# Float64 weights to float32 in an mLSTM and MoE kernel: the three low bits made by ScalarE, two VectorE passes per weight tile

## The chip, the cores and the metric

The kernel runs on one core of a Trainium2 chip. A core has TensorE (matrix products; PE in the profile, its weight loads PEld), VectorE (DVE), ScalarE (ACT), GpSimd (POOL) and the queue of SyncE (SP) that issues transfers. Each executes its own instructions in order and waits on semaphores for the others. The metric is the device time of one execution in microseconds.

## The reference, cut to what matters

Per batch and head an mLSTM recurrence runs over 768 positions with head size 40; its outputs, 8 heads side by side (320 columns), go through a feed-forward layer with softplus:

```python
m_new = np.maximum(f_gate[:, :, t] + m, i_gate[:, :, t])
f_stab = np.exp(f_gate[:, :, t] + m - m_new)
i_stab = np.exp(i_gate[:, :, t] - m_new)
C = f_stab[...] * C + i_stab[...] * np.einsum('bhd,bhe->bhde', vt, kt)
n = f_stab[...] * n + i_stab[...] * kt
h_tilde = np.einsum('bhde,bhe->bhd', C, qt)
denom = np.maximum(np.abs(nq), 1.0)
y[:, :, t] = o * h_tilde / denom          # o = sigmoid(o_gate)
...
h = x @ w_in                              # 3072 x 320 by 320 x 2048
g = np.maximum(h, 0.0) + np.log1p(np.exp(-np.abs(h)))
return (g @ w_out).astype(np.float32)     # 2048 x 320
```

`w_in` and `w_out` arrive as float64, two 32-bit words for each weight. Every product of the feed-forward layer is made from float32 values split in two parts: a rounded part (`wih`, `woh`, `X[0:3]`, `gh`) and the rest (`wil`, `wol`, `X[3:6]`, `gl`); three products replace one.

## The kernel before, in words

**Tiles.** The tokens are cut into 24 steps of 128 (a batch and a chunk of 128 positions each, in the list `ORDER`), three steps to a tile of 384 tokens, so eight tiles `t`. The hidden layer is cut into 16 blocks `f` of 128. For each pair of tile and block, `products()` issues eight matmuls into `hp` (L971) and, two blocks later, nine into the three accumulators `po` (L939); ScalarE makes `gh` and the full softplus from `hp` (L845, L846) and VectorE the rest `gl` (L849).

**The recurrence.** For each step VectorE scans the decays (`pw`, L430, two scans over 128 x 512), TensorE makes the scores `sp` (L504), VectorE multiplies them in (L506). TensorE makes the chunk's contribution `cp` to the state (L481) from `vw`, which GpSimd makes (L457) from VectorE's weights `gw` (L451); VectorE adds it to the state `cn` (L486), which the next step of that batch reads (`ip` L528, `iq` L557). The first six steps ("plain") lead to token rows `x` (L550) that TensorE transposes into `xp` (L615, L617), ScalarE casts to `X` (L619) and VectorE subtracts (L621); later steps ("wide") come out transposed (`y` L560, `yq` L568).

**The weights.** Each of 16 weight tiles (eight of `w_in`, called `i`, and eight of `w_out`, called `o`; 128 partitions x 640 weights) is loaded raw into one of three buffers `wr` (`load_weights`, L221 to L227) and turned into float32 in `single` (L190 to L207). `hi_w` and `lo_w` are the upper and lower words, read with a stride of two words. ScalarE reads `hi_w` as a float32 and scales it by 2^-112 (`mag`, L198): that moves the exponent. VectorE takes the sign bit out of `hi_w` into `sg` (L201), ORs in `mag` shifted left by three (L203), and ORs in the three top bits of `lo_w` (L205). Then ScalarE casts the result to the rounded part (L236, L240 for `w_in`, L251 for `w_out`), and GpSimd subtracts that for the rest (L243, L245, L253). `sg` has three buffers, `mag` two.

**What sets the order.** `in_order()` fixes the order of instructions on each engine as they are written. They are written by a queue of generators keyed by the count of matmuls issued: `convert(u, i)` makes one step of `single` and of what follows it at each of the offsets `CW` (for `w_in`) or `CO` (for `w_out`), `fetch` loads the next raw tile. `single` has four steps before the change and four after, so each of them falls at the same count as before. All sixteen conversions end within the first quarter of the run; from then on the weights are resident. An instruction that waits holds up all those behind it on its engine.

The first tile's start is written out by hand in `first_tile()`, which calls the first conversion (`wparts`) between the steps of the recurrence.

Of the kernel before, what the change touches and what calls it, by code (L numbers as in the profile page):

```python
# [11 lines left out]
AF = mybir.ActivationFunctionType  # L12
ALU = mybir.AluOpType
# [26 lines left out]
def mlstm_moe_kernel(  # L40
# [10 lines left out]
    nc = tc.nc  # L51
# [138 lines left out]
    def single(src, n):  # L190

        if not words:
            return src
        lo_w, hi_w = src[:, :, :, 0], src[:, :, :, 1]
        shape = list(hi_w.shape)
        mag = stage.tile(shape, F32, tag="mag", bufs=MB, name=f"mag{n}")

        nc.scalar.activation(mag, hi_w.bitcast(F32), AF.Copy, scale=2.0**-112)  # L198
        yield
        sg = stage.tile(shape, U32, tag="sg", bufs=3, name=f"sg{n}")  # L200
        nc.vector.tensor_scalar(sg, hi_w, 0x80000000, None, op0=ALU.bitwise_and)  # L201
        yield
        nc.vector.scalar_tensor_tensor(sg, mag.bitcast(U32), 3, sg, op0=ALU.logical_shift_left, op1=ALU.bitwise_or)  # L203
        yield
        nc.vector.scalar_tensor_tensor(sg, lo_w, 29, sg, op0=ALU.logical_shift_right, op1=ALU.bitwise_or)  # L205
        yield
        return sg.bitcast(F32)  # L207

# [21 lines left out]
    def weights(u):  # L230

        cs = slice(u * 256, (u + 1) * 256)
        w = yield from single(raw[u, 0], f"i{u}")
        w2 = w[:, 0:4].rearrange("p (c j) f -> p c (j f)", c=2)
        los = []
        nc.scalar.copy(wih[:, 0:2, cs], w2)  # L236
        for i in range(2):
            c1 = slice((2 * u + i) * 128, (2 * u + i + 1) * 128)
            hi, lo = slice(i * 64, (i + 1) * 64), slice((1 - i) * 64, (2 - i) * 64)
            nc.scalar.copy(wih[hi, 2, c1], w[hi, 4])  # L240
            los.append((wih[lo, 2, c1], w[hi, 4], wih[hi, 2, c1]))
        yield
        nc.gpsimd.tensor_tensor(wil[:, :, cs], w2, wih[:, 0:2, cs], op=ALU.subtract)  # L243
        for d, x, y in los:
            nc.gpsimd.tensor_tensor(d, x, y, op=ALU.subtract)  # L245
        yield

    def weights_out(u):
        w = yield from single(raw[u, 1], f"o{u}")
        js = slice(2 * u, 2 * u + 2)  # L250
        nc.scalar.copy(woh[:, js, :], w)  # L251
        yield
        nc.gpsimd.tensor_tensor(wol[:, js, :], w, woh[:, js, :], op=ALU.subtract)  # L253
        yield
# [842 lines left out]
```

## Time and profile before

| | |
|---|---|
| three runs | 496.26, 500.42 and 500.45 us, median 500.42 |
| the profiled execution | 497.97 us, of which 496.3 between its first and last instruction (the span) |
| mean granted TensorE clock in it | 0.974 |
| busy in the span | TensorE 473.9 us (96%), weight loads 451.9, VectorE 336.3 (68%), GpSimd 223.4 (45%), ScalarE 205.8 (41%) |
| the five instruction lines that convert weights on VectorE and ScalarE | L198 12.6 us, L201 12.1, L203 16.5, L205 17.3; the casts L236, L240, L251 15.5 |

How to read the views in the prediction. A row of stretches gives the start and end of a stretch in us from the span's start, its length, then the busy us of PE, PEld, DVE, ACT and POOL (with the count of instructions that start in it), the granted clock (1.00 is full), the DMA share and GB/s. A row of a timeline gives start, duration, engine, line, operation, output and inputs, shape and count; the bracket is the idle time of that engine before it and what ended it. A grouped row gives busy us, mean ns and the idle time before. A row of a line gives the shortest, median and longest duration in ns. A row of waits gives the total, how often, and the longest.

### The profile page before, as it was taken

The numbers are of one execution on the slowest core, as the hardware profiler recorded it, in microseconds if no ns is written. First come the engines' busy times: TensorE is split into PE (matmuls) and PEld (weight loads), VectorE is DVE, ScalarE is ACT, GpSimd is POOL, SyncE is SP. The second block draws the span as 40 slices with busy tenths as digits, with TensorE's granted clock in tenths as the row PEclk, the third lists the DMA queues.
The fourth block names the chain that finished last, engine by engine and source line by source line (L and its number), as shares of the span: only waits on it lengthen the run. The fifth ranks groups of instructions, "written<-read, shape, count | busy, mean of one in ns | idle before, by whom it ended". The sixth has DMA issues, their size and how long they took to land.

```text
span 496.3 us, 9355 instructions
## 1 busy us (share of the span) xinstructions
PE 473.9 (96%) x3444; PEld 451.9 (91%) x3444; DVE 336.3 (68%) x533; ACT 205.8 (41%) x408; POOL 223.4 (45%) x303
## 2 busy tenths in 40 slices
PE   8988979798999989999999999999999999999996
PEld 8977878697998889999999999999999999999996
DVE  8788967888877576696587677578568657542211
ACT  2544515376424632536343534254352632333332
POOL 8256736666966324743365352643374344010000
PEclk9997978989999999999999999999999999999999
DMA  6936873769865877568856684569655572001001
GB/s 181 302 119 199 245 220 97 201 169 276 216 179 142 243 205 206 163 177 210 220 154 178 193 227 140 168 192 221 205 155 183 149 210 71 16 22 42 0 1 40
DMA packets 52991, 81.10 MB, mean 163 GB/s; under 512 B 7906, under 2 KB 31634, under 8 KB 52946
## 3 DMA queue, kind: packets, MB, share of 16 engines
q1 hardware_dynamic: 44738, 67.82, 49.0%
q0 software_dynamic: 4320, 8.26, 6.1%
q10 hardware_dynamic: 3888, 4.43, 2.8%
q8 instruction: 27, 0.44, 0.4%
q14 instruction: 18, 0.15, 0.1%
HBM read 52.38 MB, written 8.80 MB: 123 GB/s over the span
## 4 chain that ended last, share of the span: by engine, by line
PE 70%; DMA 12%; DVE 11%; issue 3%; ACT 2%; SPq 1%; POOL 0%; ACTq 0%; DVEq 0%; POOLq 0%
PE hp L971 31%; PE po L939 29%; PE yq L568 3%; PE sp L504 3%; DVE pw L430 3%; DMA wr<-in_w_in 3%; PE cp L481 2%; PE iq L557 2%; DMA wo<-in_w_out 2%; DMA out<-ob 1%; DMA sgp<-og 1%; DMA kst<-in_qk 1%; DMA fb<-fz_d 1%; DVE sgo L203 1%; DMA qst<-in_qk 1%
## 5 line engine op out<-in xcount | busy, mean ns | idle before, releaser
L971 PE MATMUL hp<-X,wih 128*128 128x384 f32 x768 | 185.3, 345 | 4.4 <-ACT X L619 3.0
L971 PEld LDWEIGHTS hp<-X,wih 128*128 128x128 f32 x768 | 133.8, 191 | 7.4 <-ACT X L619 3.4
L845 ACT ACTIVATE gh<-hp 128x384 fp32r<-128x384 f32 x128 | 62.7, 490 | 173.1 <-PE hp L971 154.5
L849 DVE TENSOR_TENSOR gl<-hp,gh 128x384 fp32r<-128x384 f32 x128 | 70.2, 549 | 58.1 <-ACT hp L846 57.8
L939 PE MATMUL po<-woh,gh 128*128 128x320 f32 x384 | 84.3, 318 | 0.1
L939 PE MATMUL po<-woh,gl 128*128 128x320 f32 x384 | 83.5, 312 | 0.1
L939 PE MATMUL po<-wol,gh 128*128 128x320 f32 x384 | 83.0, 316 | 0.0
L430 DVE TENSOR_TENSOR_SCAN pw<-fb,ident 128x512 f32<-128x512 f32 x48 | 73.2, 1565 | 0.1
L971 PE MATMUL hp<-X,wil 128*128 128x384 f32 x256 | 70.7, 349 | 0.3 <-POOL wil L243 0.3
L939 PEld LDWEIGHTS po<-woh,gh 128*128 128x128 f32 x384 | 66.8, 192 | 0.9 <-ACT gh L845 0.4
L939 PEld LDWEIGHTS po<-wol,gh 128*128 128x128 f32 x384 | 62.9, 191 | 1.0 <-issue 0.9
L939 PEld LDWEIGHTS po<-woh,gl 128*128 128x128 f32 x384 | 62.8, 189 | 0.6 <-DVE gl L849 0.4
L846 ACT ACTIVATE hp<-hp 128x384 f32<-128x384 f32 x128 | 62.3, 486 | 0.0
L580 POOL DMA_DIRECT2D yd<-y x36 | 20.8, 579 | 89.3 <-DVE y L573 87.5
L971 PEld LDWEIGHTS hp<-X,wil 128*128 128x128 f32 x256 | 46.8, 192 | 1.8 <-issue 1.0
L560 DVE TENSOR_TENSOR y<-iq,y 41x512 f32<-41x512 f32 x36 | 24.6, 682 | 28.3 <-PE iq L557 25.5
L504 PEld LDWEIGHTS sp<-qst,kst 120*128 120x128 f32 (+1 forms) x240 | 34.4, 202 | 3.6 <-DVE pw L506 1.3
L504 PE MATMUL sp<-qst,kst 120*128 120x128 f32 (+1 forms) x240 | 34.9, 281 | 2.5 <-DVE pw L506 1.1
L605 ACT CAST X<-eg 128x384 fp32r<-128x384 f32 x18 | 9.2, 514 | 58.8 <-DVE eg L603 58.8
L506 DVE TENSOR_TENSOR pw<-sp,pw 128x512 f32<-128x512 f32 x48 | 31.8, 680 | 2.3 <-PE sp L504 2.1
L457 POOL TENSOR_TENSOR vw<-vt,gw 128x328 f32<-128x328 f32 x19 | 15.8, 835 | 36.2 <-DVE gw L451 26.7
L486 DVE TENSOR_TENSOR cn<-cn,cp 40x328 f32<-40x328 f32 x16 | 7.8, 486 | 32.8 <-POOL cn L472 32.8
(131 smaller groups left out, 603.0 us busy)
## 6 DMA issues: line engine op xcount, KB each, us to landing
fb<-fz_d SPq DMA_DIRECT2D x42, 256.0 KB
vt<-in_vko SPq DMA_DIRECT2D x23, 324.0 KB
qst<-hiq SPq DMA_DIRECT2D x36, 160.0 KB
kst<-hik SPq DMA_DIRECT2D x36, 160.0 KB
wo<-in_w_out SPq DMA_DIRECT2D x8, 640.0 KB
wr<-in_w_in SPq DMA_DIRECT2D x8, 512.0 KB
eg<-in_oT SPq DMA_DIRECT2D x6, 576.0 KB
yd<-y POOLq DMA_DIRECT2D x36, 96.0 KB, 3.6
```

Of the source, the lines that this page charges most:

```text
L430: nc.vector.tensor_tensor_scan(pw.rearrange(flat), fb.rearrange(flat), ident4.rearrange(flat), 0.0, ALU.mult, ALU.add)
L457: nc.gpsimd.tensor_tensor(z.vw, v1, z.gw.broadcast_to([128, H, E]), op=ALU.mult)
L504: nc.tensor.matmul(sp[:, j, :], z.kst[:, h, :], z.qst[:, h, :], start=True, stop=True)
L506: nc.vector.tensor_tensor(z.pws[i], sp, z.pws[i], op=ALU.mult)
L560: nc.vector.tensor_tensor(y, iq, y, op=ALU.mult)
L568: nc.tensor.matmul(yq[e0:e1, p, :], z.via[:, h * E : h * E + e1 - e0], z.pws[h // HG][:, h % HG, :], start=True, stop=True)
L580: nc.gpsimd.dma_start(rows[i], z.y[i * PP : i * PP + EP])
L845: nc.scalar.activation(gh, hp, AF.Softplus)
L846: nc.scalar.activation(hp, hp, AF.Softplus)
L849: nc.vector.tensor_tensor(gl, hp, gh, op=ALU.subtract)
L939: nc.tensor.matmul(po[j], a[:, j * 128 : (j + 1) * 128], w[:, f, :], start=(first and left[j] == 2), stop=(last and left[j] == 0),)
L971: nc.tensor.matmul(hp, a, r, start=(i == 0), stop=(i == len(seq) - 1))
```

## The change

ScalarE makes the three low bits: it reads `lo_w` as a whole number, multiplies by 2^-29, subtracts 0.4375 and writes a whole number into `sg`, which rounds to the number in the top three bits (for the uppermost sixteenth of each interval to the next one, a difference at the last bit of the weight's precision). VectorE then takes sign and low bits together in one pass, and ORs in `mag` shifted by three as its second and last. The pass that took the sign alone is gone.

```diff
         sg = stage.tile(shape, U32, tag="sg", bufs=3, name=f"sg{n}")
-        nc.vector.tensor_scalar(sg, hi_w, 0x80000000, None, op0=ALU.bitwise_and)
+        nc.scalar.activation(sg, lo_w, AF.Copy, scale=2.0**-29, bias=-0.4375)
+        yield
+        nc.vector.scalar_tensor_tensor(sg, hi_w, 0x80000000, sg, op0=ALU.bitwise_and, op1=ALU.bitwise_or)
         yield
         nc.vector.scalar_tensor_tensor(sg, mag.bitcast(U32), 3, sg, op0=ALU.logical_shift_left, op1=ALU.bitwise_or)
-        yield
-        nc.vector.scalar_tensor_tensor(sg, lo_w, 29, sg, op0=ALU.logical_shift_right, op1=ALU.bitwise_or)
         yield
         return sg.bitcast(F32)
```

In the changed kernel L201 is ScalarE's pass, L203 VectorE's first and L205 its second. TensorE, GpSimd and SP keep their instructions and their order. Two places on the other engines matter for the prediction.

VectorE around the conversion `sgo_587` (about 46 to 51 us), before:

```order
L205 SCALAR_TENSOR_TENSOR sgi_478<-wr_392,sgi_478 128x640
L201 TENSOR_SCALAR sgo_587<-wo_461 128x640
L849 TENSOR_TENSOR gl_2_590<-hp_2_514,gh_2_561 128x384
L203 SCALAR_TENSOR_TENSOR sgo_587<-mago_570,sgo_587 128x640
L205 SCALAR_TENSOR_TENSOR sgo_587<-wo_461,sgo_587 128x640
L201 TENSOR_SCALAR sgi_645<-wr_521 128x640
L430 SCALAR_TENSOR_TENSOR pw_1_0_649<-fb_1_0_543,ident_79 128x512
```

and now:

```order
L205 SCALAR_TENSOR_TENSOR sgi_478<-magi_476,sgi_478 128x640
L849 TENSOR_TENSOR gl_2_590<-hp_2_514,gh_2_561 128x384
L203 SCALAR_TENSOR_TENSOR sgo_587<-wo_461,sgo_587 128x640
L205 SCALAR_TENSOR_TENSOR sgo_587<-mago_570,sgo_587 128x640
L430 SCALAR_TENSOR_TENSOR pw_1_0_649<-fb_1_0_543,ident_79 128x512
```

Two passes are gone ahead of the scan L430. The first pass of `sgo_587` now reads what ScalarE wrote.

ScalarE at the same conversion, now:

```order
L198 ACTIVATE mago_570<-wo_461 128x640
L236 CAST wih<-sgi_478 128x2x256
L240 CAST wih<-sgi_478 64x128 x2
L201 ACTIVATE sgo_587<-wo_461 128x640
L845 ACTIVATE gh_3_615<-hp_3_593 128x384
L846 ACTIVATE hp_3_593<-hp_3_593 128x384
L251 CAST woh<-sgo_587 128x640
```

The row of L201 is new, the others stand as before. It comes behind the casts of the tile before, `sgi_478`, which need VectorE's last pass on that tile. The same pattern stands at `sgo_720` and `sgo_865`; in the other conversions L201 stands directly behind L198, or behind other activations.

ScalarE at the third X cast of the second tile (about 96 us), what the change adds there:

```order
 L846 ACTIVATE hp_9_1006<-hp_9_1006 128x384
 L251 CAST woh<-sgo_992 128x640
 L198 ACTIVATE magi_1042<-wr_757 128x640
+L201 ACTIVATE sgi_1044<-wr_757 128x640
 L619 CAST X_761<-xp_2_1046 128x3x128
 L845 ACTIVATE gh_0_1063<-hp_0_1041 128x384
```

The new pass stands between L198 and the X cast.

## The prediction

> **What bounds the kernel now.** I read the stretches first (busy time of each engine between two times, then the granted TensorE clock, the DMA share and GB/s), because the conversion of the weights happens only in the first 130 us and an average over 496 us hides it.
>
> ```profile
> 26.00:30.00 4.00, 1.91 (x15) 1.37 (x14) 2.30 (x3) 1.59 (x5) 1.29 (x2) 1.00 0.23 56
> 38.00:40.00 2.00, 0.86 (x9) 0.67 (x8) 1.89 (x4) 0.00 (x0) 0.00 (x0) 1.00 0.40 69
> 40.00:48.00 8.00, 7.75 (x42) 6.86 (x43) 5.68 (x11) 4.13 (x11) 6.63 (x9) 0.57 0.81 237
> 66.00:78.00 12.00, 11.31 (x55) 10.80 (x55) 7.83 (x14) 2.09 (x5) 3.10 (x5) 0.57 0.45 132
> 98.00:102.00 4.00, 4.00 (x16) 3.98 (x16) 2.11 (x3) 0.87 (x2) 0.46 (x1) 0.57 0.90 271
> 122.00:126.00 4.00, 4.00 (x16) 4.00 (x17) 3.97 (x5) 1.94 (x5) 3.86 (x4) 0.57 0.92 195
> 300.00:480.00 180.00, 180.00 (x1298) 174.97 (x1297) 105.97 (x172) 70.50 (x146) 59.43 (x92) 1.00 0.42 119
> ```
>
> From 300 to 480 us TensorE (first busy figure) has work all the time at full clock: nothing is to be had there. What can be saved lies before 130 us, in two kinds. TensorE idles, and in four stretches it runs at a mean clock of 0.57. The second loss is 0.43 of 8, 12, 4 and 4 us: 3.4, 5.2, 1.7 and 1.7, together 12.0 us. The first is read in TensorE's own timeline, where a bracket gives the idle time ahead of a row and its releaser:
>
> ```profile
> 27.80 0.41 PE L615 MATMUL xp<-ident,x 128*128 128x128 f32 x2 [1.75 <-DVE x L550]
> 39.67 0.30 PE L177 MATMUL pg<-ident,d 32*128 32x32 f32 x2 [1.14 <-DVE d L168]
> 43.01 1.01 PE L971 MATMUL hp<-X,wil 128*128 128x384 f32 x2 [0.25 <-POOL wil L243]
> 57.49 1.16 PE L504 MATMUL sp<-qst,kst 128*128 128x128 f32 x8 [1.07 <-DVE pw L506]
> 65.55 1.98 PE L528 MATMUL ip<-cn,qst 128*128 128x42 f32 x16 [1.89 <-DVE cn L486]
> 84.57 1.98 PE L528 MATMUL ip<-cn,qst 128*128 128x42 f32 x16 [0.42 <-DVE cn L486]
> 94.03 0.41 PE L615 MATMUL xp<-ident,x 128*128 128x128 f32 x2 [0.45 <-DVE x L550]
> 97.42 1.33 PE L971 MATMUL hp<-X,wih 128*128 128x384 f32 x4 [2.62 <-ACT X L619]
> 117.47 0.43 PE L557 MATMUL iq<-qst,cs 120*41 120x128 f32 x4 [0.36 <-DVE cn L486]
> 120.83 1.08 PE L568 MATMUL yq<-pw,vi 128*64 128x128 f32 x16 [1.99 <-DVE y L560]
> 132.13 0.78 PE L481 MATMUL cp<-vw,vt 128*40 128x41 f32 x16 [0.43 <-POOL vw L457]
> ```
>
> These eleven waits are 12.4 us. Eight end with VectorE, two with GpSimd (which itself waited for VectorE or ScalarE) and one, the longest, with ScalarE. So VectorE's queue sets the pace here, and a pass taken out of it counts only where it stands ahead of such a release.
>
> **The change, part by part.** Price of the pass that goes, and of the one that comes:
>
> ```profile
> L201 DVE TENSOR_SCALAR sgo<-wo 128x640 uint32<-128x640 uint32 x8 | 6.2, 777 | 0.0
> L201 DVE TENSOR_SCALAR sgi<-wr 128x640 uint32<-128x640 uint32 x8 | 5.9, 742 | 0.0
> L198 ACT ACTIVATE mago<-wo x8: 767/792/803, 30.7 to 125.2; 128x640 f32<-128x640 f32 x8
> ```
>
> *Removed:* sixteen sign passes (L201), 6.2 + 5.9 = 12.1 us of VectorE. The last column says that none of them waited. *Changed:* the first of the two passes left reads the raw word and the tile `sg`, the second `mag` and `sg`: two tensors each, as L203 and L205 do now, so I give them no new price. *Added:* sixteen low-bit passes on ScalarE. The trace has no such activation with whole numbers in and out; nearest is L198, which reads the same tile with the same stride and size: 0.79 us. The bound below is 0.73, the L251 cast of the same size (row at 95.60 further down); above I take twice L198, 1.58, an estimate for conversion at half rate. I take 0.79. ScalarE gets 12.7 us more, in a stretch where it is mostly half idle (4.13 of 8 us, 2.09 of 12).
>
> A rule of the Trainium skill speaks against this trade. The page ScalarE: Activation LUTs, section Rules for kernel authors, sends multiplying and adding to VectorE, not ScalarE, as VectorE is the quicker per element. The trace agrees only in part: the rows give 0.78 and 0.74 for the pass removed and 0.79 for the one added. By the rule the move would be a loss wherever ScalarE is the one waited for; by the rows it is an even exchange of busy time.
>
> Now place by place, with the sign passes that stand ahead of a release:
>
> ```profile
> 24.52 0.48 DVE L201 TENSOR_SCALAR sgi<-wr 128x640 uint32<-128x640 uint32 x1
> 30.48 0.70 DVE L201 TENSOR_SCALAR sgi<-wr 128x640 uint32<-128x640 uint32 x1
> 32.10 1.02 DVE L201 TENSOR_SCALAR sgo<-wo 128x640 uint32<-128x640 uint32 x1
> 47.10 1.03 DVE L201 TENSOR_SCALAR sgo<-wo 128x640 uint32<-128x640 uint32 x1
> 51.07 0.74 DVE L201 TENSOR_SCALAR sgi<-wr 128x640 uint32<-128x640 uint32 x1
> 59.41 1.04 DVE L201 TENSOR_SCALAR sgo<-wo 128x640 uint32<-128x640 uint32 x1
> 63.89 0.74 DVE L201 TENSOR_SCALAR sgi<-wr 128x640 uint32<-128x640 uint32 x1
> 90.41 0.44 DVE L201 TENSOR_SCALAR sgo<-wo 128x640 uint32<-128x640 uint32 x1
> 117.34 0.48 DVE L201 TENSOR_SCALAR sgo<-wo 128x640 uint32<-128x640 uint32 x1
> 119.61 0.49 DVE L201 TENSOR_SCALAR sgi<-wr 128x640 uint32<-128x640 uint32 x1
> 128.27 0.68 DVE L201 TENSOR_SCALAR sgo<-wo 128x640 uint32<-128x640 uint32 x1
> ```
>
> - *Wait at 27.80.* One pass of 0.48 goes, but the low-bit pass now stands between two X casts on ScalarE and delays the second. Taken: 0.25.
> - *39.67.* Two passes, 1.72 us, go ahead of the scans and of L168. The wait of 1.14 closes: 1.1. The rest turns into slack.
> - *43.01.* GpSimd's subtraction stands behind the same VectorE work: 0.25.
> - *57.49.* Two passes go, 1.03 and 0.74. But the wait that the change adds shows here. In the new ScalarE order the low-bit pass of `sgo_587` follows the casts of `sgi_478`, and these wait for the last VectorE pass of `sgi_478`:
>
> ```profile
> 47.20 0.77 ACT L198 ACTIVATE mago<-wo 128x640 f32<-128x640 f32 x1
> 47.87 0.61 ACT L236 CAST wih<-sgi 128x512 fp32r<-128x512 f32 x1
> 48.38 0.62 ACT L240 CAST wih<-sgi 64x128 fp32r<-64x128 f32 x2
> ```
>
>   The casts end at 49.00, the low-bit pass at 49.8; VectorE, which would be at that first pass at 47.10 + 0.54 (the `gl` subtraction between), stands still for about 2 us less what moved up, say 1.4. Queued behind it on VectorE are the second pass, the two scans and L506, and for that TensorE waits. Taken: 1.77 - 1.4 = 0.4.
> - *65.55.* Same pattern at `sgo_720`, but `gl` and L506 stand between the casts' release and the waiting pass; the stall is 1.9 - 1.1 = 0.8, and 1.04 + 0.74 go. Taken: 0.8, cautiously, as parts of a pass overlap the next row.
> - *84.57 and 94.03.* One pass each stands ahead: 0.42 (the whole wait) and 0.35 (of 0.44).
> - *97.42.* Here ScalarE is late, and the change makes it later:
>
> ```profile
> 95.60 0.73 ACT L251 CAST woh<-sgo 128x640 fp32r<-128x640 f32 x1 [2.37 <-DVE sgo L205]
> 96.23 0.78 ACT L198 ACTIVATE magi<-wr 128x640 f32<-128x640 f32 x1
> 96.92 0.45 ACT L619 CAST X<-xp 128x384 fp32r<-128x384 f32 x1
> ```
>
>   The X cast that TensorE waits for follows the L198 of `sgi_1044`, and the change puts that tile's low-bit pass between them: 0.7 later (0.79 less the overlap of neighbours: 96.23 + 0.78 ends past 96.92). This is a loss of 0.7.
> - *117.47, 120.83, 132.13.* 0.3 (of 0.48), then 0.4: passes of 0.48 and 0.49 go, but the low-bit pass of `sgo_1255` comes before the activations of the next block, and VectorE waits some 0.5 for it; then 0.43, the whole last wait, as 0.68 goes ahead of the weights `gw` that GpSimd multiplies by. Together 1.1.
>
> Sum of the waits: 0.25 + 1.1 + 0.25 + 0.4 + 0.8 + 0.42 + 0.35 - 0.7 + 1.1 = 4.0 us (3.97). So a third of the 12.1 us of VectorE arrives at TensorE. The rest was never ahead of a release, fills stalls on ScalarE, or goes into VectorE's own waits for TensorE. If TensorE is earlier by 4.0 at 132 us it stays so, since behind it the work is TensorE's own: the row of 300 to 480 us.
>
> *Edits at nothing.* GpSimd, SP and TensorE keep their order. The ring of three `sg` buffers is now waited for by ScalarE, not VectorE; the 0.0 in the L201 rows is the cover (the buffer was always free in time). Without it, ScalarE would hold back the activations behind it; a wait of 1 us for each of two would eat half the sum. `mag` is held one pass longer, 0.8 us; the next L198 into the same buffer comes behind casts that wait for that pass anyway. The raw words are let go one or two passes earlier: rival 3.
>
> *The clock.* The bound above a gain is all 12.0 us; below, the loss of another stretch like that of 66 to 78 us, 5.2. Every slow stretch stands behind a wait: 1.14, 1.89, 2.62, 1.99. But waits of 1.75 and 1.07 led to none, so it is chance in part which wait costs one. Of the four, the change closes the 1.14, shrinks 1.89 to 1.1 and 1.99 to 1.6, and lengthens 2.62 to 3.3. I count half of the stretch whose wait closes: 3.4 / 2 = 1.7.
>
> The Trainium skill (TensorE: Matmul & The Clock Gate, Part 1: The HAM clock gate) has the clock drop to half after about 3.4 us of idling in a free-running window. The lengths agree (losses of 1.7, 3.4 and 5.2 are one, two and three windows at half clock), but here waits of 1.14 to 2.62 us were enough; the measurement decides. By the rule as written no wait left would drop it, by the rows some will.
>
> **Sum.** The profiled execution took 497.97 (span 496.3, 1.7 around it). 497.97 - 4.0 - 1.7 = 492.3 us. The three runs shown have a median of 500.42 and a lowest of 496.26, so the profiled one lies 2.45 below the median; I keep the sum and let the range carry that.
>
> **Rivals.**
>
> 1. *The stalls give it all back.* VectorE's first pass now waits for ScalarE, whose low-bit pass waits behind casts that wait for VectorE. If the stall is 2 us in each of the two places above, the gains of 0.4 and 0.8 are gone; if the low-bit pass takes 1.58 the X cast is 0.8 later yet. 4.0 - 1.2 - 0.8 = 2.0, no change of clock: 496.0, and up to 500 in an execution like the two upper runs. Against the median of 500.42 that is within 1%, about what a measurement of this kernel can tell from no change. For it: ScalarE executes in order. Against: in most conversions its low-bit pass comes directly behind L198, long before VectorE needs it.
>
> 2. *ScalarE's queue becomes the bound: slower.* The mechanism is the X cast at 97.42 met at each conversion of an output tile: the casts (1.1), the low-bit pass (0.8) and then VectorE's two passes in strict turn, where one sign pass of 0.78 stood before. Each of eight costs 1.9 - 0.78 = 1.1, if nothing stands between: 8.8, less the 2.2 that the eight other passes would still give at the share of a third (5.9 / 3, and 0.25): 6.6, and one more stretch of clock, 1.7: 497.97 + 6.6 + 1.7 = 506.3. It decides once more than about six of the eight meet the stall in full. For it: the two new orders read above. Against: only three low-bit passes stand behind such casts, and 40 to 48 and 66 to 78 us leave ScalarE half idle.
>
> 3. *More than the sum: earlier loads and a quiet clock.* The raw words are released after VectorE's first pass instead of its last, and SP issues everything in order behind this wait:
>
> ```profile
> SPq L227 <- DVE sgi L205: 11.2, 1, 11.2
> ```
>
>    If the transfers of the next step behind it come earlier too, and both long clock stretches go (3.4 + 5.2): 497.97 - 4.0 - 8.6 = 485.4. For it: SP's 11.2. Against: no TensorE row above names a DMA.
>
> 4. *The clock goes on as it was.* The stretches belong to the windows and not to the waits I close: 497.97 - 4.0 = 494.0. This is the forecast's lower gain and is counted with it. That the change does not do what it says is small: the order shows sixteen passes gone and sixteen come; only the ScalarE price is unknown, and stands in rival 1.
>
> **How the numbers follow.** Forecast with rival 4, 0.40; rival 1, 0.37; rival 3, 0.12; rival 2, 0.11. Predicted time 492.3. The range begins at 487, leaving out about half of rival 3, and ends at 501, above rival 1 with the 2.45 and a little noise, leaving out rival 2: together some 0.2. Faster by over 1% (below 495.4): forecast and rival 3, 0.52. Within 1%: rival 1, 0.37. Slower: 0.11.
>
> **What would show it.** Right: L201 on ScalarE at 0.79, sixteen times; no wait at L177; L486 ahead of the wait at 65.55 some 2 to 4 us earlier; VectorE rows that wait for L201 near 48 and 61 us by 0.8 to 1.4; the X cast at 97 with a longer wait; 12 us less VectorE busy time and an unchanged stretch from 300 us on. Wrong: low-bit passes well over 0.8, waits of ScalarE for GpSimd at L201, or TensorE's waits closed and the total unchanged, which would mean that the wait is taken back by a transfer or the clock after 132 us.

## The result, and the profile after

The changed kernel takes 496.18 us (median of 20 runs, 492.68 to 500.39) against 499.77 for the kernel before (20 runs, 496.26 to 504.77): ratio 0.9922, 95% interval 0.9901 to 0.9943, so 0.8% faster, 3.6 us. A second comparison (e12 below) gave 0.9944, 0.9909 to 0.9979. The 496.18 is inside the predicted range and 3.9 us above the predicted 492.3. The profiled execution took 494.4, with a span of 492.7 and a mean granted clock of 0.981 (before: 497.97, 496.3, 0.974). The ratios on record, here and below, leave out the few runs over 1.5% above the fastest of their kernel (one of the 20 here, two of the six of e9), and can differ by up to 0.5% from the quotient of the medians of all runs.

The groups by line first, of the changed kernel (busy us, mean ns of one | idle time ahead and what ended it):

```profile
L203 DVE SCALAR_TENSOR_TENSOR sgo<-wo,sgo 128x640 uint32<-128x640 uint32 x8 | 8.7, 1088 | 4.7 <-ACT sgo L201 2.7 <-POOL wil L243 2.1
L203 DVE SCALAR_TENSOR_TENSOR sgi<-wr,sgi 128x640 uint32<-128x640 uint32 x8 | 8.7, 1088 | 0.9 <-ACT sgi L201 0.9
L201 ACT ACTIVATE sgo<-wo 128x640 uint32<-128x640 uint32 x8 | 6.3, 787 | 0.1
L201 ACT ACTIVATE sgi<-wr 128x640 uint32<-128x640 uint32 x8 | 6.3, 785 | 0.0
```

The low-bit pass (L201) costs 0.79 us, as taken. VectorE's busy time falls by 11.7 us (336.3 to 324.6), ScalarE's rises by 10.5 (205.8 to 216.3). New is the last column of L203: VectorE now stands idle for 5.6 us ahead of its first pass.

TensorE's timeline of the changed kernel, the rows with an idle time that answer to those of before:

```profile
27.22 0.41 PE L615 MATMUL xp<-ident,x 128*128 128x128 f32 x2 [1.09 <-DVE x L550]
38.83 0.31 PE L177 MATMUL pg<-ident,d 32*128 32x32 f32 x2 [0.84 <-DVE d L168]
42.13 1.01 PE L971 MATMUL hp<-X,wil 128*128 128x384 f32 x2 [0.87 <-POOL wil L243]
56.54 1.16 PE L504 MATMUL sp<-qst,kst 128*128 128x128 f32 x8 [0.54 <-DVE pw L506]
63.71 1.98 PE L528 MATMUL ip<-cn,qst 128*128 128x42 f32 x16 [0.99 <-DVE cn L486]
78.55 1.98 PE L528 MATMUL ip<-cn,qst 128*128 128x42 f32 x16 [0.61 <-DVE cn L486]
94.73 1.60 PE L971 MATMUL hp<-X,wih 128*128 128x384 f32 x4 [3.27 <-ACT X L619]
114.22 0.44 PE L557 MATMUL iq<-qst,cs 120*41 120x128 f32 x4 [0.29 <-DVE cn L486]
117.12 1.08 PE L568 MATMUL yq<-pw,vi 128*64 128x128 f32 x16 [1.53 <-DVE y L560]
123.59 0.64 PE L504 MATMUL sp<-qst,kst 120*128 120x128 f32 x4 [2.20 <-DMA lok<-in_qk]
```

Most waits for VectorE are shorter, but three rows wait longer (42.13, 78.55 and 94.73; the first ends with GpSimd, the last with ScalarE) and the last row is new: the same scores started at 126.50 before, without a wait. Read the left column as well: the gain, row by row against before, is 0.6 at 27 us, 0.8 at 39, 0.9 at 42, 1.0 at 57, 1.8 at 64, 6.0 at 79, 2.7 at 95, 3.7 at 117, then 2.9 at 124. The 6.0 is in large part the clock: before, a slow stretch lay between 66 and 78 us, now one lies between 78 and 94. From there to the end of the span it is 369.1 us here and 369.8 before.

And the stretches (busy time of each engine, then TensorE's granted clock, DMA share, GB/s):

```profile
40.00:48.00 8.00, 7.13 (x38) 6.58 (x35) 4.21 (x7) 4.72 (x13) 6.92 (x10) 0.57 0.82 232
66.00:78.00 12.00, 11.59 (x89) 9.90 (x87) 10.61 (x17) 4.60 (x10) 7.72 (x9) 1.00 0.66 191
78.00:94.00 16.00, 12.92 (x69) 12.00 (x69) 8.04 (x13) 7.57 (x13) 9.21 (x7) 0.79 0.59 191
122.00:126.00 4.00, 2.41 (x17) 2.44 (x18) 3.96 (x4) 1.69 (x4) 3.85 (x4) 1.00 0.80 192
300.00:480.00 180.00, 180.00 (x1287) 175.36 (x1287) 104.55 (x169) 71.19 (x148) 59.77 (x92) 1.00 0.41 115
```

The stretch of 40 to 48 us is as slow as before (0.57). That of 66 to 78 us is gone, but one stands at 78 to 94 (0.21 of 16 is 3.4 us lost, 5.2 before); that of 122 to 126 is gone. The one behind the X cast costs 1.7 us, as before (0.64 over 94 to 98 us and 0.93 over 98 to 102). From 300 us on TensorE is busy all the time at full clock, as before. Over the span the clock's loss is (1 - 0.981) x 492.7 = 9.4 us against 12.9 before: in this one pair the 3.6 us is about what the clock gave back.

One pair is not enough to say so, since each execution draws its own stretches and waits. So for each kernel I split every run's span in the same way: the loss by the clock, (1 - granted clock) x span, and the rest, span x clock, and take means over the runs. It is a rough split (a slow clock costs nothing while TensorE idles anyway), but it is the same for all. It takes every run.

| kernel (runs) | ratio to before [95%] | loss by clock, us | rest, us |
|---|---|---|---|
| before (92, in three sets) | 1 | 13.1 | 484.3 |
| change (20) | 0.9922 [0.9901, 0.9943] | 10.4 | 484.0 |
| e12 change again (12) | 0.9944 [0.9909, 0.9979] | 11.7 | 483.2 |
| e1 no ScalarE pass (11) | 0.9913 [0.9877, 0.9950] | 9.5 | 483.0 |
| e2 ScalarE pass alone (12) | 1.0069 [1.0036, 1.0102] | 15.1 | 485.2 |
| e3 low bits early, output tiles (12) | 0.9925 [0.9895, 0.9955] | 10.9 | 482.6 |
| e4 raw words let go early (12) | 0.9985 [0.9957, 1.0013] | 12.4 | 483.6 |
| e5 low bits late, input tiles (12) | 0.9947 [0.9916, 0.9977] | 10.8 | 483.3 |
| e6 raw words held (12) | 0.9983 [0.9945, 1.0021] | 11.7 | 484.4 |
| e7 four VectorE passes (6) | 1.0233 [1.0189, 1.0277] | 18.5 | 489.6 |
| e8 extra matmuls in a wait (12) | 0.9938 [0.9902, 0.9973] | 9.0 | 485.1 |
| e9 one VectorE pass (6) | 0.9768 [0.9716, 0.9819] | 6.6 | 481.9 |
| e10 last load late (12) | 0.9931 [0.9904, 0.9958] | 10.2 | 484.2 |
| e11 three moves (12) | 0.9945 [0.9913, 0.9977] | 12.0 | 483.0 |

The standard error of a mean is some 0.2 to 0.8 us for rows with 11 to 20 runs, but 1.05 for the loss of e11; for e7 it is 1.2 and 0.7, for e9 1.8 and 0.3. Over its 32 runs the change lost 2.2 us (error 0.4) less to the clock and has 0.5 (error 0.3) less of the rest.

### The profile page after: what moved, and what is told of

It is laid out like the page before. It is cut to its first block, busy times and chain, and to the rows that moved or that the text cites. A ratio compares the mean times of both kernels' runs of the same rounds, so it can differ in the third digit from the quotient of the medians.

```text
span 492.7 us, 9346 instructions
## 1 busy us (share of the span) xinstructions
PE 471.5 (96%) x3444; PEld 449.2 (91%) x3444; DVE 324.6 (66%) x517; ACT 216.3 (44%) x424; POOL 222.6 (45%) x303
## 4 chain that ended last, share of the span: by engine, by line
PE 74%; DVE 10%; DMA 6%; ACT 4%; issue 3%; POOL 1%; SPq 1%; ACTq 0%; DVEq 0%; POOLq 0%
PE hp L971 32%; PE po L939 30%; PE yq L568 4%; PE sp L504 3%; PE cp L481 2%; DVE pw L430 2%; PE iq L557 2%; PE yp L538 1%; DMA og<-in_vko 1%; DMA nw<-yd 1%; DMA yd<-y 1%; DVE sgo L203 1%; DMA vt<-in_vko 1%; DMA y<-fc_d 1%; DVE sgi L205 1%
## 5 line engine op out<-in xcount | busy, mean ns | idle before, releaser
L430 DVE TENSOR_TENSOR_SCAN pw<-fb,ident 128x512 f32<-128x512 f32 x48 | 72.3, 1545 | 0.2 <-PE fb L416 0.2
L504 PEld LDWEIGHTS sp<-qst,kst 120*128 120x128 f32 (+1 forms) x240 | 33.2, 196 | 4.7 <-issue 3.5
L504 PE MATMUL sp<-qst,kst 120*128 120x128 f32 (+1 forms) x240 | 33.8, 275 | 3.7 <-DMA lok<-in_qk 2.2
L486 DVE TENSOR_TENSOR cn<-cn,cp 40x328 f32<-40x328 f32 x16 | 7.8, 486 | 32.2 <-POOL cn L472 32.2
```

Source lines behind the costliest of these rows:

```text
L430: nc.vector.tensor_tensor_scan(pw.rearrange(flat), fb.rearrange(flat), ident4.rearrange(flat), 0.0, ALU.mult, ALU.add)
L504: nc.tensor.matmul(sp[:, j, :], z.kst[:, h, :], z.qst[:, h, :], start=True, stop=True)
```

## The experiments: what is VectorE's pass worth, and ScalarE's?

**e1, the relief of VectorE alone.** The ScalarE pass is left out; this kernel leaves out the three low bits of each weight.

```diff
-        nc.scalar.activation(sg, lo_w, AF.Copy, scale=2.0**-29, bias=-0.4375)
+
...
-        nc.vector.scalar_tensor_tensor(sg, hi_w, 0x80000000, sg, op0=ALU.bitwise_and, op1=ALU.bitwise_or)
+        nc.vector.scalar_tensor_tensor(sg, hi_w, 0x80000000, hi_w, op0=ALU.bitwise_and, op1=ALU.bitwise_and)
```

> The changed kernel without its ScalarE pass: VectorE's first pass takes the sign of the upper word from two reads of that word, so price and place of both passes stay, nothing waits for ScalarE, and the three low bits of each weight are left out. My theory (VectorE relief is the gain, ScalarE gives part of it back: 3.6 us of VectorE waits for L201 and 0.65 us at the X cast in the changed kernel's trace): 2 us below the changed kernel, about 494 where that is 496.2, ratio to before 0.988. Rival (the gain is the earlier release of the raw words, or the clock alone): as the changed kernel, 0.992.

Measured: 493.38 against 499.08, ratio 0.9913. So even with nothing put on ScalarE, one VectorE pass less per tile brings 0.5 to 1.2%. It is not the change's VectorE without the waits: VectorE is busy for 327.7 us here, 324.6 in the change, since the 32 passes left take 35.6 us in place of 34.2. TensorE's rows of this kernel:

```profile
94.73 1.21 PE L971 MATMUL hp<-X,wih 128*128 128x384 f32 x4 [2.63 <-ACT X L619]
123.26 0.64 PE L504 MATMUL sp<-qst,kst 120*128 120x128 f32 x4 [3.69 <-DMA loq<-in_qk]
```

The X cast's wait is back at the 2.6 of before, so the 0.65 that the change adds there is the low-bit pass. The wait for transfers near 123 us is there without the ScalarE pass too, so ScalarE is not needed for it. How the low-bit pass rounds, which the section on the change describes, no run here measures. Whether the change is slower than e1 can't be said: the intervals overlap.

**e2, ScalarE's work alone.** The kernel before, with the pass that makes `mag` made twice.

```diff
         nc.scalar.activation(mag, hi_w.bitcast(F32), AF.Copy, scale=2.0**-112)
         yield
+        nc.scalar.activation(mag, hi_w.bitcast(F32), AF.Copy, scale=2.0**-112)
```

> The kernel before, with its three VectorE passes, and a second identical L198 pass on ScalarE directly before each L201: the price of sixteen ScalarE passes of 0.79 us alone. My theory: half hidden, plus 1 us, ratio 1.002 (0.7 of it at the third X cast of the second tile). Rival (ScalarE's queue is close to the bound, my rival 2): plus 4 us or more, 1.008 and up. Rival (ScalarE has room everywhere): 1.000.

Measured: 502.16 against 499.08, ratio 1.0069. Sixteen passes on an engine that is 41% busy cost some 3 us (0.4 to 1.0%). Where:

```profile
L199 ACT ACTIVATE mago<-wo 128x640 f32<-128x640 f32 x8 | 6.3, 794 | 0.2
L199 ACT ACTIVATE magi<-wr 128x640 f32<-128x640 f32 x8 | 6.3, 790 | 0.2
```

```profile
38.71 0.49 PE L175 MATMUL pg<-ident,ig 32*128 32x32 f32 x5 [1.15 <-ACT cn L488]
100.39 1.65 PE L971 MATMUL hp<-X,wih 128*128 128x384 f32 x4 [3.43 <-ACT X L619]
```

The pass has the price of the low-bit pass (0.79). TensorE's wait for the X cast is 0.8 longer, one pass; a wait for a ScalarE copy of `cn` is new; and VectorE, which reads what the added pass writes, waits 3.1 us for it. Only 0.9 (error 0.5) of the cost is in the rest, 2.0 (error 0.6) in the clock. So the added pass isn't free in the kernel before. That it eats as much of the relief in the change is not shown: the ratios of e1 and the change overlap.

**e7, one VectorE pass more.** The kernel before, with the sign pass made twice.

```diff
         nc.vector.tensor_scalar(sg, hi_w, 0x80000000, None, op0=ALU.bitwise_and)
+        nc.vector.tensor_scalar(sg, hi_w, 0x80000000, None, op0=ALU.bitwise_and)
```

> The kernel before with the sign pass (L201) made twice at once, so VectorE takes four passes for a tile instead of three: 12.1 us more of VectorE, 16 passes of 0.76. Theory (a third of VectorE's time arrives at TensorE, as the prediction had it): 4.0 us slower without the clock, ratio 1.008, and the eleven TensorE waits grow by about 4. Rival (VectorE's weight passes are not ahead of what sets the end; what the change won is clock alone): net time (time less the loss by the clock) within 1 us of before, ratio 0.998 to 1.003.

Measured: 510.06 against 499.01, ratio 1.0233: 11 us, far over both expectations. The trace has 9.6 us more of VectorE (336.3 to 345.9), so the time grows by more than that; but only half is work or waiting. The rest is 5.4 us longer (error 0.7), somewhat over the 4.0 of the first theory, and the clock loses another 5.3 (error 1.2).

```profile
58.94 1.16 PE L504 MATMUL sp<-qst,kst 128*128 128x128 f32 x8 [1.61 <-DVE pw L506]
65.25 0.78 PE L481 MATMUL cp<-vw,vt 128*40 128x41 f32 x16 [1.70 <-POOL wih L245]
122.17 0.78 PE L481 MATMUL cp<-vw,vt 128*40 128x41 f32 x16 [3.38 <-POOL cn L472]
```

The first wait is 0.5 longer than in the kernel before; the other two are new: GpSimd, which takes what VectorE makes (`wih` from `sgi` in L245), is late now.

**e9, one VectorE pass less.** The change without its first pass; this kernel leaves out the signs of the weights.

```diff
-        nc.vector.scalar_tensor_tensor(sg, hi_w, 0x80000000, sg, op0=ALU.bitwise_and, op1=ALU.bitwise_or)
+
```

> The changed kernel without its first VectorE pass (L203, the sign): one pass of VectorE is left for a tile, 12 us less again. It leaves out the signs of the weights. Runs so far: four passes cost 11 us more than three, two passes without ScalarE's save 4.8. Theory (two passes are at the corner: what TensorE waits for then is the X cast on ScalarE and the transfers, which a further pass does not move): at most 2 us under the change, ratio 0.988 to 0.992, with the waits at L971 (X) and for a DMA near 123 us still there. Rival (VectorE still paces, a pass is worth at least the 4 to 5 us that the last one was): ratio 0.984 or less and those waits shorter.

Measured: 490.31 against 499.54, 6 us under the change on the same chip (496.61). These medians of all runs give 0.982, the ratio on record is 0.9768; its six runs lie far apart, from 484.45 to 495.5. By either figure my theory of a corner at two passes falls: a further pass is worth as much as the last one or more. But TensorE's waits stand at the places that the theory named:

```profile
90.97 1.65 PE L971 MATMUL hp<-X,wih 128*128 128x384 f32 x4 [3.26 <-ACT X L619]
118.88 0.63 PE L504 MATMUL sp<-qst,kst 120*128 120x128 f32 x4 [2.06 <-DVE pw L430]
```

The long wait for the X cast stands and only comes earlier. The second is put down to VectorE, not to a transfer. The rest falls by 1.3 us (error 0.6) against the change on that chip, the clock's loss by 5 (error some 1.9). So the time falls with every VectorE pass taken out (medians over those of before: 1.022 with four, 1, 0.993 and 0.994 with two, 0.982 with one), and at each step about half of what a pass is worth or more is the clock. TensorE multiplies other numbers in e9, all weights positive; whether the clock follows the numbers was not tested.

## The experiments: where the gain was lost

**e3 and e5, the place of the low-bit pass on ScalarE.** In e3 it comes earlier for output tiles, ahead of the casts of the tile before; in e5 later for input tiles, behind the third X cast.

```diff
-    CO = [0, 5, 8, 12, 17, 22]
+    CO = [0, 0, 8, 12, 17, 22]
```

> The changed kernel with the low-bit pass of the output tiles written directly behind L198, ahead of the casts that wait for VectorE (CO second entry 0 for 5). My theory: the waits of VectorE for L201 on output tiles (2.7 us by the trace, four times) go, and 1 to 1.5 us come back: 495, ratio to before 0.990. Rival (those waits are covered by TensorE's own work or by the clock): as the changed kernel, 0.992.

```diff
-    CW = [-4, -15, 8, 12, 13, 26]
+    CW = [-4, 0, 8, 12, 13, 26]
```

> The changed kernel with the due time of the low-bit pass of the input tiles at 0 in place of -15: ScalarE makes this pass some operations later, and at the third X block it stands behind the X cast (L619) and not ahead of it. Theory: TensorE's wait for that cast, 3.27 us in the changed kernel, is 0.7 longer than it need be; it goes back to about 2.5 and the time falls by 0.7: ratio to the kernel before 0.991 where the change has 0.992. If the slow-clock stretch behind this wait goes as well, another 1.7: 0.987. Rival: the wait is only moved, since the tile's VectorE passes become later by as much and the next casts with them: ratio 0.992 or more, and the first hp rows after 94 us no earlier than in the change.

Measured: 0.9925 and 0.9947, both like the change. Yet each did what it should at its place. The wait of VectorE for the low bits of output tiles (2.7 in four places, and the 2.1 put down to GpSimd, which is gone) in e3:

```profile
DVE sgo L203 <- ACT sgo L201: 1.3, 2, 0.8
```

and TensorE's wait for the X cast (3.27) in e5:

```profile
94.55 1.21 PE L971 MATMUL hp<-X,wih 128*128 128x384 f32 x4 [2.36 <-ACT X L619]
128.03 0.81 PE L481 MATMUL cp<-vw,vt 128*40 128x41 f32 x16 [1.38 <-POOL vw L457]
```

What was taken away there is not seen in the time. In e3 VectorE's passes take it back: all its waits ahead of L203 fall from 5.6 us to 2.5, but the 32 weight passes take 37.7 us in place of 34.2. At `sgo_587` the pass ahead of the former stall takes 2.04 us (0.84 in the change), the one behind it 1.78 (0.97), and the scan, which now waits 0.79 us for a transfer, starts only 0.3 us earlier. In e5 VectorE's waits grow to 6.5, and a wait for GpSimd stands at 128 us that the change has not. The rest is 0.5 and 1.1 us less than in the change (errors 0.6), hardly over its error.

**e4 and e6, when the raw words are let go.** e4 is the kernel before with its last two passes swapped, so that the raw buffer is free one pass earlier; e6 is the change with its two passes swapped, so that it is held to the last pass as before.

```diff
-        nc.vector.scalar_tensor_tensor(sg, mag.bitcast(U32), 3, sg, op0=ALU.logical_shift_left, op1=ALU.bitwise_or)
+        nc.vector.scalar_tensor_tensor(sg, lo_w, 29, sg, op0=ALU.logical_shift_right, op1=ALU.bitwise_or)
         yield
-        nc.vector.scalar_tensor_tensor(sg, lo_w, 29, sg, op0=ALU.logical_shift_right, op1=ALU.bitwise_or)
+        nc.vector.scalar_tensor_tensor(sg, mag.bitcast(U32), 3, sg, op0=ALU.logical_shift_left, op1=ALU.bitwise_or)
```

> The kernel before with its last two VectorE passes in the other order, so that the raw words are released one pass earlier, and nothing else. My theory: no change, ratio 1.000. Rival 3 of the prediction (earlier loads carry the gain): a third to a half of the gain, ratio 0.996.

```diff
-        nc.vector.scalar_tensor_tensor(sg, hi_w, 0x80000000, sg, op0=ALU.bitwise_and, op1=ALU.bitwise_or)
+        nc.vector.scalar_tensor_tensor(sg, mag.bitcast(U32), 3, sg, op0=ALU.logical_shift_left, op1=ALU.bitwise_or)
         yield
-        nc.vector.scalar_tensor_tensor(sg, mag.bitcast(U32), 3, sg, op0=ALU.logical_shift_left, op1=ALU.bitwise_or)
+        nc.vector.scalar_tensor_tensor(sg, hi_w, 0x80000000, sg, op0=ALU.bitwise_and, op1=ALU.bitwise_or)
```

> The changed kernel with its two VectorE passes in the other order, so that the raw words are read by the last pass again and their buffer is let go as late as before the change. Theory: the earlier release lets the loads of the next tile (L277) start 4 to 6 us earlier, ahead of what TensorE's scores near 123 us need, and made the new wait of 2.20 us there (sp<-qst,kst for a DMA); with the late release that wait is gone and the time falls by 1 to 2 us: ratio 0.988 to 0.990. Rival: the wait only stands for VectorE being earlier there (TensorE arrives sooner at a transfer that lands when it lands), so that the time is that of the change: 0.992, with the wait still there or replaced by one for VectorE.

Measured: 0.9985 and 0.9983, neither told from 1. I had blamed the early release for the new wait for a transfer. It is not the cause, since with the late release the wait is still there:

```profile
127.23 1.08 PE L504 MATMUL sp<-qst,kst 120*128 120x128 f32 x4 [5.33 <-DMA lok<-in_qk]
```

The 5.33 here against 2.20 does not show that the early release shortens the wait: a second profile of the change itself has 4.21 there (e12 below). Nor can the gain of e6 be told from nothing, or from that of the change, since its interval (0.9945 to 1.0021) overlaps that of e12. That the early release helps the change is likely by the middle values, not shown.

**e10, the wait for transfers taken away.**

```diff
-        yield (CO if i else CW)[3] + 8
+        yield (CO if i else CW)[3] + 8; yield -1000 - 20 * (len(raw) == NF - 1)
```

> The changed kernel with the load of the last output weight tile (wo, 640 KB, issued at 112.17 us) put off, so that SP issues it behind the four small loads of qst, kst and cn that TensorE's scores near 123 us need. Theory: the new wait of 2.20 us there stands for the DMA engines being full (share 0.91 to 1.04 from 108 to 124 us) and 640 KB at some 250 GB/s are 2.5 us: the wait goes, and the time falls by 1 to 2: ratio 0.988 to 0.990. Rival: the wait passes to the next one behind it (y from VectorE, or the weights themselves, which now come late near 130 us): ratio 0.992 or more.

Measured: 0.9931, like the change. TensorE's scores in that place, and its next wait:

```profile
122.88 0.56 PE L504 MATMUL sp<-qst,kst 120*128 120x128 f32 x4
```

```profile
129.65 0.81 PE L481 MATMUL cp<-vw,vt 128*40 128x41 f32 x16 [1.64 <-POOL vw L457]
```

The scores ran at 122.88 with no wait. So the 640 KB ahead of their loads were the cause: e11, with the same edit, has no wait there either, and the seven profiles of two passes without it have one of 0.7 to 5.3 us. But 7 us later TensorE waits 1.64 for `vw`. GpSimd makes it at 128.86, right behind its own work (until 128.79); VectorE's `gw`, behind two scans and two weight passes, was ready at 128.36. The rival's reading holds, though with another next wait than it named: near 130 us several chains end close together.

**e11, three moves together.** The edits of e3, e5 and e10.

> The changed kernel with three moves of order together: the low-bit pass of output tiles as early as mag (ahead of the casts of the tile before), that of input tiles later (behind the X cast), and the last weight load put off as in the run on that alone. Theory: each takes away one of the waits that ate the gain (VectorE's for the low bits, the X cast's 0.7, the transfer's 2.2), so together 2 to 4 us under the change: ratio 0.984 to 0.988. Rival: the places follow one another with slack in between and the clock is chance, so it stays within 1 us of the change: 0.990 to 0.994.

Measured: 0.9945. The three waits are shorter or gone at their places (VectorE's ahead of L203 4.2 us for 5.6, the X cast 2.60, the transfer none), but VectorE's 32 passes take 36.9 us for 34.2, and TensorE waits 2.46 us for `vw` at 130.46. The rest, 483.0, is not told from the change's. No version here with the full computation is shown to beat the change.

**e12, the change again.**

> The changed kernel itself, on the same chip as the three others of this batch, for comparison with them: ratio 0.990 to 0.994 as before if the result holds from chip to chip. Its loss by the clock should be some 2 to 3 us under that of the kernel before, and the rest of its time within 1 us of it.

Measured: 496.61 against 499.54, ratio 0.9944. Its profiled execution has a span of 499.1, 6.4 us more than the first one of the same program:

```profile
96.64 1.65 PE L971 MATMUL hp<-X,wih 128*128 128x384 f32 x4 [3.28 <-ACT X L619]
127.56 1.09 PE L504 MATMUL sp<-qst,kst 120*128 120x128 f32 x4 [4.21 <-DVE sgo L203]
```

The X wait is the same (3.28). The wait at 127.56 is 2.0 longer, and the clock's loss is (1 - 0.972) x 499.1 = 14.0 instead of 9.4. Those two, 2.0 and 4.6, are about the 6.4. The wait is put down to a weight pass that the scores do not read, and ended when that pass did; what released it in truth I can't say.

**e8, work in a wait.** Do TensorE's waits bring the slow clock? The change, with twelve matmuls of the identity in the longest wait.

```diff
             X = Xs[t]
+            [nc.tensor.matmul(hp[:, :128], ident, ident, start=True, stop=True) for r in range(12 * ((t, f) == (1, 0)))]
```

> The changed kernel with twelve extra 128x128 matmuls of the identity into hp ahead of the first block that needs the third X (L959; the block's first matmul then overwrites them), so that TensorE has about 2.6 us of work in its wait of 3.27. Nothing is computed differently. Theory (waits cause the slow clock): the slow stretch behind this wait, 3.4 us long at half clock, does not come, and the loss by the clock falls by up to 1.7 us in the mean of the runs: ratio 0.989. Rival (the clock does not follow single waits): loss as in the change, 10.4, and ratio 0.992 to 0.994, above it where the extra matmuls run past the cast.

Measured: 0.9938, the time of the change. At the place, TensorE's timeline and the stretch behind it in e8:

```profile
94.04 2.94 PE L959 MATMUL hp<-ident 128*128 128x128 f32 x24
97.43 1.21 PE L971 MATMUL hp<-X,wih 128*128 128x384 f32 x4 [0.44 <-ACT X L619]
```

```profile
98.00:102.00 4.00, 4.00 (x25) 3.98 (x25) 2.35 (x4) 1.20 (x3) 0.00 (x0) 1.00 0.87 262
```

and the same stretches in e12, whose wait there is 3.28:

```profile
96.00:98.00 2.00, 1.36 (x4) 1.27 (x5) 1.29 (x2) 0.58 (x2) 0.49 (x1) 0.53 0.78 210
98.00:102.00 4.00, 4.00 (x22) 4.00 (x22) 1.43 (x3) 0.98 (x3) 0.00 (x0) 0.81 0.79 233
```

The wait shrinks to 0.44 and the slow clock behind it does not come. The other profiles agree: of those with 3.26 to 3.43 us of wait at this cast (the change, e2, e3, e6, e9, e10, e12) all seven have a stretch at half clock around or right behind it, of those with 2.08 to 2.63 (before, e1, e4, e5, e7, e11) four of six. In the mean the loss is 9.0 (error 0.8) against 10.9 over the 32 runs of the change, in line with the 1.7 of one such stretch but only two errors away. The rest is higher by 1.3 (error 0.7), and no time is won. That a wait brings the slow clock is made likelier, not shown; why the rest is higher stays open.

## Why the prediction was right, and where it was off

**Total.** Forecast: 5.7 us off a profiled execution of 497.97. Measured between medians: 3.6, and 2.9 in the second comparison. Of the 3.9 us between 492.3 and 496.18, 1.8 is the base: that execution lay 1.8 under the median of 499.77. The other 2.1 is a gain taken too large. The forecast of a gain of over 1% was not met: 0.8 and 0.6%. The range of 14 us was wide enough to hold rival 1 as well, so that the time fell into it says little for the forecast. By the split of the table over the 32 runs, 0.5 (error 0.3) of the forecast 4.0 came outside the clock, and 2.2 (error 0.4) as clock, where 1.7 was forecast.

**The price of the passes** was right: 0.785 and 0.787 us on ScalarE in the mean, 0.83 at most, and 11.7 us less of VectorE. The Trainium skill's rule against the trade (ScalarE: Activation LUTs, Rules for kernel authors) is borne out in part. The means of 0.78 and 0.74 make it an even exchange, but the sign passes with no GpSimd tensor work beside them took 0.48 to 0.49 us (10 passes in four profiles), so VectorE is the quicker where it is undisturbed; and e2 shows that passes put on ScalarE cost some 3 us.

**The sum of waits, 4.0, is the step that was off.** Without the clock, TensorE was 2.0 us earlier at 117 us (3.7, less 1.7 for the slow clock up to there), where my terms add up to 3.5. By row: 27.80 gave 0.6 (I took 0.25); 57.49 0.5 (0.4); 65.55 0.9 (0.8); 94.03 0.45 (0.35); 97.42 lost 0.65 (0.7). The list of eleven waits also left out three (0.36 at 30.03, 0.69 at 69.11, 0.53 at 110.87). Four terms went wrong:

- *39.67, 1.1 taken, 0.30 measured.* From the subtraction of X to the start of the scan L168, which ends the wait, VectorE took 8.14 us before, 7.87 in the change and 7.61 in e1, which has no pass on ScalarE:

```profile
30.00 0.56 DVE L621 TENSOR_TENSOR X<-xp,X 128x384 fp32r<-128x384 f32 x1 [1.70 <-ACT X L619]
38.14 1.48 DVE L168 TENSOR_TENSOR_SCAN d<-fg,d 32x640 f32<-32x640 f32 x1
```

```profile
29.43 0.56 DVE L621 TENSOR_TENSOR X<-xp,X 128x384 fp32r<-128x384 f32 x1 [1.71 <-ACT X L619]
37.30 1.48 DVE L168 TENSOR_TENSOR_SCAN d<-fg,d 32x640 f32<-32x640 f32 x1
```

```profile
29.80 0.56 DVE L621 TENSOR_TENSOR X<-xp,X 128x384 fp32r<-128x384 f32 x1 [1.70 <-ACT X L619]
37.41 1.48 DVE L168 TENSOR_TENSOR_SCAN d<-fg,d 32x640 f32<-32x640 f32 x1
```

  So 0.27 of the 1.72 us of passes taken out arrive, the rest of the 0.84 by which the row is earlier came from 27.80. A part went into a stall: the one that I costed at `sgo_587` and `sgo_720` has a third place, which I had not costed. VectorE's timeline of the change at the three:

```profile
30.91 1.36 DVE L203 SCALAR_TENSOR_TENSOR sgi<-wr,sgi 128x640 uint32<-128x640 uint32 x1 [0.93 <-ACT sgi L201]
49.04 0.83 DVE L203 SCALAR_TENSOR_TENSOR sgo<-wo,sgo 128x640 uint32<-128x640 uint32 x1 [2.05 <-POOL wil L243]
60.56 1.22 DVE L203 SCALAR_TENSOR_TENSOR sgo<-wo,sgo 128x640 uint32<-128x640 uint32 x1 [0.96 <-ACT sgo L201]
```

  and ScalarE's ahead of each:

```profile
28.92 0.48 ACT L619 CAST X<-xp 128x384 fp32r<-128x384 f32 x1
29.42 0.79 ACT L198 ACTIVATE magi<-wr 128x640 f32<-128x640 f32 x1
30.12 0.77 ACT L201 ACTIVATE sgi<-wr 128x640 uint32<-128x640 uint32 x1
48.17 0.78 ACT L201 ACTIVATE sgo<-wo 128x640 uint32<-128x640 uint32 x1
59.75 0.79 ACT L201 ACTIVATE sgo<-wo 128x640 uint32<-128x640 uint32 x1
```

  At 30.12 both ScalarE passes stand behind an X cast, and VectorE's sign pass, which had filled that time before, is gone. But e1 has no such stall and gains only 0.53. What both lose besides is in the passes left: the three ahead of the scans took 3.6 us before (0.89, 1.35, 1.35) and 4.0 in the change (1.36, 1.25, 1.35); in e1 they took 3.7 with a wait of 0.5, and the two scans behind them 2.87 for 2.33. That the passes left need no new price, as the prediction has it, is what failed there. The other two stalls are 2.05 (I took 1.4; L201 ends at 48.95, so it is the wait that I meant, though the profile names GpSimd, whose L243 ends within 0.1 us of it) and 0.96 (0.8).

- *43.01, 0.25 taken, 0.6 lost.* GpSimd's subtraction came 0.9 earlier, like all VectorE work there, but TensorE came 1.5 earlier: in the kernel before it ran that block at half clock and arrived later. A wait that a slow clock had covered is uncovered.

- *84.57, 0.42 taken, 0.2 lost.* The wait is 0.61 now, at 78.55: with no slow stretch from 66 to 78 us TensorE came 6 us earlier, and VectorE's `cn` could not follow.

- *"If TensorE is earlier by 4.0 at 132 us it stays so."* It did not. At 123.59 it met the transfers of `qst` and `kst` and waited 2.20. I had held against rival 3 that no row of TensorE names a DMA; but a row shows only the last to come, and with VectorE's part earlier the loads are last. The first of these loads, before and now:

```profile
117.50 0.73 SPq L390 DMA_DIRECT2D kst<-lok  x1
```

```profile
113.38 0.73 SPq L390 DMA_DIRECT2D kst<-lok  x1
```

  It was issued 4.1 us earlier, while TensorE came 5.1 earlier (121.39 for 126.50); and from there to the scores it is 10.2 us now, at most 9.0 before, so the loads took longer too. e10 and e11, with 640 KB moved behind the loads, have no wait there. An earlier TensorE is not the whole cause: in e2 it comes later than before, at 128.51, and waits 2.17.

**The clock** was a half counted for 1.7; the runs have 2.2 less loss in the mean. That size was luck: the stretch whose wait was to close (39.67) stayed, at 0.57 from 40 to 48 us as before, and others went. The rule cited from the Trainium skill (TensorE: Matmul & The Clock Gate, Part 1: The HAM clock gate) has the clock drop after about 3.4 us of idling; no wait in the profile of the change reaches that (the longest is 3.27), and slow stretches come all the same.

**The rivals.** Rival 1 (the stalls give it back) is nearest in time, 496.0, but only a part of its mechanism came: the stalls are 3.6 us of VectorE for L201 or, with the row at 49.04, 5.6 in all, and e3 took 3.1 of these away without a gain. Rival 2 (ScalarE the bound) did not come, though e2 has its direction. Of rival 3 the early release is real (SP's weight load L227, which waited for L205 before, waits for L203 now); that it helps is not shown by e4 and e6.

**What would show it**, point by point: L201 at 0.79 sixteen times, yes; no wait at L177, no (0.84); L486 ahead of the wait at 65.55 earlier by 2 to 4, nearly (TensorE starts there 1.8 earlier); VectorE waiting near 48 and 61 us by 0.8 to 1.4, yes and more (2.05 and 0.96); a longer X wait, yes (3.27); 12 us less VectorE, yes; unchanged from 300 us on, yes.

## What to carry to other kernels

Cost the gain as the time at which the bounding engine passes a row, carried on from row to row, and not as a sum of waits that close: what is freed early meets the next chain (a cast, a load, another engine), which had ended just behind. A pass moved to an engine that is half idle is paid for wherever it stands ahead of something waited for, so read the new order on that engine at every conversion, not at the two places that look worst. Where a pass or a stall goes, read also what now runs beside the passes left: they need not keep their price. And before a gain of under 1% is read out of one pair of profiles, look how far two profiles of one program lie apart: here 6.4 us.

## What the runs showed of the hardware that was not expected

- The loss by the clock went with the count of VectorE passes. Mean loss: 18.5 us with four passes, 13.1 with three, 10.4 and 11.7 with two (the change), 6.6 (error 1.8) with one. Of the 11 us that a fourth pass costs, 5.3 are the clock's.
- A VectorE pass that reads two tensors of a weight tile (L203, L205) has no one price. With no tensor instruction of GpSimd beside it, it took 0.80 to 0.83 us (all 103 such passes of the 14 profiles); with one beside it for more than half of its time, 0.81 to 2.27, in the mean 1.17 (260 passes).
- The activation with 32-bit whole numbers in and out, with scale and bias, takes 0.785 to 0.787 us for 128 x 640 read at a stride of two words, like the one on floats (0.79).
- Twelve 128 x 128 matmuls of the identity in float32 show as 24 records and 2.94 us at full clock, and the slow stretch behind them did not come.
